# A hashed-attention and maxout kernel: softmax sums from weights added on VectorE, PSUM copies on ScalarE, and a new sharing of the PSUM banks

## The chip, the cores and the metric

The kernel runs on one core of a Trainium2 chip. The metric is device time in microseconds (us) of one execution. The profile gives the span from the first to the last instruction of one execution. The core has five engines, each with its own queue that it works through in order: TensorE (PE in the profile; PEld are its weight loads), VectorE (DVE), ScalarE (ACT), GpSimd (POOL) and SyncE (SP, which here only starts transfers). They wait for each other through semaphores. TensorE writes its products to PSUM, eight banks of 512 single-precision columns over 128 partitions; VectorE and ScalarE read them there.

## The reference

Four batches, eight heads, 768 rows, head width 64. Each row of q and k gets a bucket from the signs of six projections, and a row attends only to rows of its own bucket. A maxout layer of three products and an output product follow.

```python
q_bits = (np.einsum('bhsd,dk->bhsk', q, proj) > 0)
k_bits = (np.einsum('bhsd,dk->bhsk', k, proj) > 0)
...
mask = q_bucket[:, :, :, None] == k_bucket[:, :, None, :]
scores = np.where(mask, scale * np.matmul(q, k.transpose(0, 1, 3, 2)), -1000000000.0)
attn = np.exp(scores - np.max(scores, axis=-1, keepdims=True))
attn = attn / (np.sum(attn, axis=-1, keepdims=True) + 1e-09)
x = np.matmul(attn, v)        # to (4*768, 512)
h = np.maximum(np.maximum(x @ w1, x @ w2), x @ w3)
out = h @ w_out               # 512 -> 768 -> 512
```

## The kernel before

**The mask is in the product.** The hash bits, as plus and minus one half, stand as six or eight more rows under the 64 rows of q and k (tiles S). The score product then carries the match of the bits, and the exponential on ScalarE (L257) with a bias makes weights of unlike buckets vanish.

**Units.** The work is a loop over 192 units `u`, 48 for each batch. A unit is one head, half of the queries (384 columns) and two blocks of 128 keys: two products on TensorE (`scores`, L255) into a two-bank PSUM tile, and one exponential of 128 x 768 on ScalarE into a half-precision tile AT, of which there are 18 (`at_tiles`). Three units make the six key blocks of one head; six make a group (two heads, half of the queries).

**Order.** It is written out by hand (`manual_schedule`). In each pass of the loop stand, in this order: `scores(u + 1)`, work due at that unit (`when`), the scaling of finished groups (`steps`), one piece of the layers (`ffn.pop(0)()`), and the values and sums of finished groups (`firsts` in the first batch, `burst` every 12 units after it).

**Values and sums.** `values(g)` (L281) multiplies the weights with v, 24 products on four strips of 32 columns of the array, four at a time. `part_sums` (L337; L308 for two groups) multiplies them with ones for the row sums, again 24 products for two groups. VectorE copies the values out of PSUM (L330). `inverse` (L291 to L294, VectorE) makes reciprocals, which GpSimd spreads over partitions (L343 to L347), and L351 writes the scaled values to xT, the layers' input. A burst runs values, sums, the hash of a coming set, values, and `invert`.

**Layers.** For each half batch there are 18 first-layer groups of four products (L366), in turn for w1, w2 and w3: VectorE casts the first product to the tile ht (L370) and takes maxima with the other two (L372). Then six half groups of three products (L399) make three output blocks, which ScalarE copies out (L403); SP sends them. The pieces run one in a unit. Those of the last half batches run on after the last scores and make the tail. L385 and L387 copy the halves of the very last block.

**Inputs.** The first batch's pairs of heads come over TensorE transposes (L111, kept by VectorE at L117, placed by GpSimd at L122) and a hash (L133, L153). Later sets of four heads (`load_quad`, L170) come as four transfers, each over 32 partitions; VectorE transposes them in 32 x 32 blocks (L176, eight for a pair of sets), GpSimd narrows them to bf16 (L181), SP places them (L187), and TensorE hashes them (L197). From the third batch on GpSimd's queue issues the loads.

**PSUM.** Two score tiles of two banks (`sc_ps`), one bank for values (`av_ps`) and three banks in rotation (`ms_ps`) for all else: eight banks. Each request makes a new tile, and the framework adds the waits that its earlier use makes needful.

```python
sc_ps = ctx.enter_context(tc.tile_pool(name="sc_ps", bufs=2, space=bass.MemoryType.PSUM))
av_ps = ctx.enter_context(tc.tile_pool(name="av_ps", bufs=1, space=bass.MemoryType.PSUM))
ms_ps = ctx.enter_context(tc.tile_pool(name="ms_ps", bufs=3, space=bass.MemoryType.PSUM))
```

Of the kernel before, what the change touches and what calls it, by code (L numbers as in the profile page):

```python
# [17 lines left out]
def kernel(  # L18
# [38 lines left out]
    nat_pool = ctx.enter_context(tc.tile_pool(name="nat", bufs=6))  # L57
# [24 lines left out]
    wout_sb = konst.tile([P, NFB, DM], FP16, name="wout_sb")  # L82

# [40 lines left out]
    def pair_group(pi, side, hd):  # L124
        mp = ms_ps.tile([P, 512], FP32, tag="ms", name="mp")
        pair_keep(pi, side, hd, pair_turn(pi, side, hd, mp))

    def pair_hash(pi):
        bp = ms_ps.tile([P, 512], FP32, tag="ms", name="bp")
# [33 lines left out]
    def load_quad(side, g, xs, eng):  # L163
        if (side, g) not in nat:
            start_set((side, g), [(side, 4 * g + x) for x in range(4)])
        for x in xs:
            b, h = divmod(4 * g + x, H)
            src = (q, k)[side][b, h].rearrange("(cc t m) d -> t cc (m d)", cc=CC, t=Q)
            dst = nat[side, g][x * Q : (x + 1) * Q, :].rearrange("t (cc w) -> t cc w", cc=CC)
            eng.dma_start(dst, src)  # L170
# [7 lines left out]
    def narrow(name, u):  # L178
        if name not in t16:
            t16[name] = t16_pool.tile([P, 2, S], BF16, tag="T16", name="T16")  # L180
        nc.gpsimd.tensor_scalar(out=t16[name][:, u, :], in0=t32[name][:, u, :], scalar1=RS, scalar2=1.0,  # L181
                                op0=AluOp.mult, op1=AluOp.mult)
# [7 lines left out]
    def quad_hash(g):  # L190
        bp = ms_ps.tile([P, 512], FP32, tag="ms", name="bp")
# [8 lines left out]
        nc.vector.tensor_scalar(out=bits[:], in0=bp[:, 0:HALF], scalar1=0.0, scalar2=0.5,  # L200
                                op0=AluOp.is_gt, op1=AluOp.subtract)
# [44 lines left out]
    def scores(u):  # L246
# [5 lines left out]
        sc = sc_ps.tile([P, 2, 512], FP32, tag="sc", name="sc")  # L252
# [20 lines left out]
    def values(g):  # L273
        b, qh, jj = groups[g]
        av = av_ps.tile([P, 512], FP32, tag="av", name="av")
# [21 lines left out]
    def near(g):  # L297
        avs = []

        def part_values():  # L300
            avs.append(values(g))

        def part_sums():
            av = avs[0]
            sm = ms_ps.tile([P, 512], FP32, tag="ms", name="sm")
# [14 lines left out]
    def far(gs):  # L320
        avs, sms, sb = [], [], []

        def part_values(i):
# [4 lines left out]
            av = values(gs[i])  # L328
            avs.append(avs_pool.tile([P, HALF + 4], FP32, tag="avs", name="avs"))
            nc.vector.tensor_copy(avs[i][:, 0 : HALF + 1], av[:, 0 : HALF + 1])  # L330
            nc.gpsimd.tensor_scalar_mul(sv[:, i : i + 1], avs[i][:, HALF : HALF + 1], EPS)  # L331

        def part_sums():
            sms.append(ms_ps.tile([P, 512], FP32, tag="ms", name="sm"))
            for m in range(NM):
                for r in range(4):
                    nc.tensor.matmul(sms[0][Q * r : Q * (r + 1), 0:HALF], ones[:, :],  # L337
                                     at_of(gs[r % 2], m, r // 2)[:, 0:HALF], start=(m == 0), stop=(m == NM - 1))

        def invert():  # L340
            rb = sb[1]
# [15 lines left out]
    def ffn_groups(h):  # L357
# [3 lines left out]
        for fb in range(NFB):  # L361
            for wi in range(3):
                def go(fb=fb, wi=wi):
                    ps = ms_ps.tile([P, 512], FP32, tag="ms", name="l1")
# [3 lines left out]
                    if wi == 0:  # L368
                        hts[fb] = h_pool.tile([P, HALF], FP16, tag="ht", name="ht")
                        nc.vector.tensor_copy(hts[fb][:], ps[:, 0:HALF])  # L370
# [6 lines left out]
        def last(part, tb):  # L377
            ps = ms_ps.tile([P, 512], FP32, tag="ms", name="l2")
# [11 lines left out]
        for tb in range(MH):  # L390
            def go2(part, tb=tb):
# [3 lines left out]
                if part == 0:  # L395
                    hts["ps"] = ms_ps.tile([P, 512], FP32, tag="ms", name="l2")
# [16 lines left out]
    with tc.manual_schedule():  # L413
# [10 lines left out]
        load_quad(1, 2, range(4), nc.sync)  # L424
# [11 lines left out]
        wp = ms_ps.tile([P, 512], FP32, tag="ms", name="wp")  # L436
# [170 lines left out]
```

## Time and profile before

| | |
|---|---|
| Time, median of three runs | 284.75 us (282.47 to 287.2) |
| Span of the profiled execution | 280.6 us; its whole time is not given apart from the three above |
| TensorE busy | 270.2 us (96%), granted clock 0.998 in the mean |
| VectorE busy | 177.3 us (63%) |
| ScalarE busy | 166.2 us (59%) |
| GpSimd busy | 106.9 us (38%) |
| Read from and written to memory | 25.17 and 6.29 MB |

In the profile's groups a row gives line, engine, operation, tiles, shapes, count, then busy time and mean duration of one in ns, then the idle time ahead of these instructions and what ended most of it. Products overlap in the array: one of 384 columns is drawn 326 ns long, though the next one starts 163 ns after it, so the distance from start to start is what a product costs. In a window's row each engine has its busy us and its count of instructions; then come TensorE's granted clock, the busy share of the transfer engines, and GB/s. In a timeline row stand the start, the length, the engine, line and operation, the count of merged instructions, and in brackets the idle time before it with what released it. In the list of waits stand who waited for whom, us in total, times, and the longest.

### The profile page before, as it was taken

The page shows a single profiled execution, that of the slowest core. Times are in us where ns is not written, and L with a number is a line of the kernel's source. Part 1 is how long each engine was busy: PE and PEld are TensorE (multiplying, and loading weights), DVE is VectorE, ACT ScalarE, POOL GpSimd, SP SyncE. Part 2 cuts the span into 40 slices and gives each one's busy share as a digit, 9 for nine tenths or more (in the row PEclk, how much of TensorE's full clock was granted, in tenths as well). Part 3 has the DMA queues.
Part 4 walks back from the last instruction along what each step waited for, and adds up shares of the span by engine and source line. Part 5 has one row for each costly group of instructions (what it writes and reads, how often), then busy time and mean ns, then how long its engine had stood idle before and what let it go on. Part 6 is the DMA issues. An engine that isn't in the chain of part 4 may idle for free.

```text
span 280.6 us, 6405 instructions
## 1 busy us (share of the span) xinstructions
PE 270.2 (96%) x2482; PEld 145.9 (52%) x2482; DVE 177.3 (63%) x383; ACT 166.2 (59%) x220; POOL 106.9 (38%) x201
## 2 busy tenths in 40 slices
PE   8899989899999999999999999999999999999994
PEld 4344433454555554555555554555555555555552
DVE  3755786786536594796536594896536673568580
ACT  2686676763858484764858484864858485910102
POOL 3455958153119096543118096633021120303000
PEclk9999999999999999999999999999999999999999
DMA  7998879974117439672117349772020001200303
GB/s 231 320 183 165 127 133 230 245 101 105 42 42 200 101 50 232 180 148 70 30 70 183 85 67 225 206 122 63 1 77 37 2 1 40 75 2 0 114 0 112
DMA packets 21877, 30.99 MB, mean 110 GB/s; under 512 B 2632, under 2 KB 17368, under 8 KB 21848
## 3 DMA queue, kind: packets, MB, share of 16 engines
q0 software_dynamic: 8640, 12.59, 24.9%
q1 hardware_dynamic: 12776, 17.49, 21.7%
q10 hardware_dynamic: 432, 0.52, 0.6%
q8 instruction: 19, 0.31, 0.5%
q14 instruction: 10, 0.08, 0.1%
HBM read 25.17 MB, written 6.29 MB: 112 GB/s over the span
## 4 chain that ended last, share of the span: by engine, by line
PE 87%; DVE 6%; ACT 2%; issue 2%; DMA 1%; POOL 0%; DVEq 0%; ACTq 0%
PE l L366 31%; PE sc L255 21%; PE av L281 12%; PE l L399 10%; PE sm L337 5%; PE bp L197 3%; ACT AT L257 2%; PE mp L111 2%; PE wp L438 1%; DVE ht L372 1%; PE bp L133 1%; PE bp L153 1%; PE sm L308 1%; DMA out_dram<-osb 1%; DVE rb L294 1%
## 5 line engine op out<-in xcount | busy, mean ns | idle before, releaser
L257 ACT ACTIVATE AT<-sc 128x768 f16<-128x768 f32 x192 | 153.4, 813 | 78.2 <-PE sc L255 78.0
L366 PE MATMUL l<-xT,w_sb 128*128 128x384 f16 x576 | 113.2, 326 | 0.7 <-DVE ht L372 0.6
L255 PE MATMUL sc<-S 72*128 72x384 bf16 (+1 forms) x384 | 93.1, 326 | 3.8 <-ACT AT L257 3.0
L366 PEld LDWEIGHTS <-w_sb 128*128 128x128 f16 x576 | 55.9, 97 | 39.1 <-issue 1.2
L372 DVE TENSOR_TENSOR ht<-ht,l 128x384 f16<-128x384 f16 x96 | 52.4, 546 | 17.0 <-PE l L366 13.8
L255 PEld LDWEIGHTS <-S 72*128 72x128 bf16 (+1 forms) x384 | 35.0, 98 | 40.1 <-issue 15.6
L331 POOL TENSOR_SCALAR sv<-avs 128x1 f32<-128x1 f32 x30 | 6.4, 213 | 95.8 <-DVE avs L330 95.7
L330 DVE COPY avs<-av 128x385 f32<-128x385 f32 x30 | 16.8, 560 | 38.3 <-PE av L281 38.3
L281 PE MATMUL av<-AT,vo 128*32 128x385 f16 x768 | 37.3, 327 | 0.0
L399 PE MATMUL l<-wout_sb,ht 128*128 128x512 f16 x138 | 36.5, 379 | 0.4 <-DVE ht L372 0.4
L370 DVE CAST ht<-l 128x384 f16<-128x384 f32 x48 | 26.2, 547 | 16.0 <-PE l L366 15.2
L403 ACT COPY osb<-l 128x512 f32<-128x512 f32 x23 | 13.4, 582 | 27.2 <-PE l L399 27.2
L281 PEld LDWEIGHTS <-vo 128*32 128x32 f16 x768 | 18.6, 96 | 16.9 <-issue 8.7
L181 POOL TENSOR_SCALAR T<-T 128x768 bf16<-128x768 f32 x24 | 21.5, 894 | 13.3 <-DVE T L176 11.9
L176 DVE STREAM_TRANSPOSE T<-nat 128x384 f32<-128x384 f32 x48 | 26.2, 558 | 0.0
L399 PEld LDWEIGHTS <-ht 128*128 128x128 f16 x138 | 13.3, 97 | 13.8 <-DVE ht L372 1.8
L351 DVE SCALAR_TENSOR_TENSOR xT<-avs,sv,rb 128x384 f16<-128x384 f32 x30 | 19.7, 656 | 0.0
L337 PE MATMUL sm<-AT,ones 128*32 128x384 f16 x360 | 17.2, 326 | 0.0
L343 POOL COPY rb<-rb 128x384 f32<-128x384 f32 x15 | 7.5, 503 | 24.0 <-DVE rb L294 24.0
L122 POOL TENSOR_SCALAR S<-T 64x768 bf16<-64x768 f32 (+1 forms) x17 | 12.8, 754 | 8.0 <-DVE T L117 6.9
L347 POOL COPY rb<-rb 32x384 f32<-32x384 f32 x30 | 15.0, 500 | 1.5
L345 POOL COPY rb<-rb 32x384 f32<-32x384 f32 x30 | 15.0, 499 | 1.5
(47 smaller groups left out, 136.5 us busy)
## 6 DMA issues: line engine op xcount, KB each, us to landing
out_dram<-osb SPq DMA_DIRECT2D x23, 256.0 KB
S<-T SPq DMA_DIRECT2D x48, 96.0 KB
vo<-in_v_dram POOLq DMA_DIRECT2D x8, 384.0 KB, 6.1
nat<-in_k_dram POOLq DMA_DIRECT2D x16, 192.0 KB, 3.6
nat<-in_q_dram POOLq DMA_DIRECT2D x16, 192.0 KB, 5.8
w_sb<-in_moe_w_dram POOLq DMA_DIRECT2D x3, 768.0 KB, 9.7
nat<-in_k_dram SPq DMA_DIRECT2D x10, 192.0 KB
nat<-in_q_dram SPq DMA_DIRECT2D x8, 192.0 KB
```

The lines of the kernel that those rows point to most:

```text
L176: nc.vector.transpose(t32[name][:, u, half * HALF : (half + 1) * HALF], i_)
L181: nc.gpsimd.tensor_scalar(out=t16[name][:, u, :], in0=t32[name][:, u, :], scalar1=RS, scalar2=1.0, op0=AluOp.mult, op1=AluOp.mult)
L255: nc.tensor.matmul(sc[:, j, 0:HALF], s_of[kn][0 : D + nb, kx, m * P : (m + 1) * P], s_of[qn][0 : D + nb, qx, qh * HALF : (qh + 1) * HALF], ...
L257: nc.scalar.activation(at_tiles[u % NAT][:, :, 0:HALF], sc[:, :, 0:HALF], ActFn.Exp, bias=-SCALE * 0.25 * nb, scale=SCALE)
L281: nc.tensor.matmul(av[hd * D + w * Q : hd * D + (w + 1) * Q, 0 : HALF + 1], vt[:, x, c * D + w * Q : c * D + (w + 1) * Q], at_of(g, m, hd) ...
L330: nc.vector.tensor_copy(avs[i][:, 0 : HALF + 1], av[:, 0 : HALF + 1])
L337: nc.tensor.matmul(sms[0][Q * r : Q * (r + 1), 0:HALF], ones[:, :], at_of(gs[r % 2], m, r // 2)[:, 0:HALF], start=(m == 0), stop=(m == NM ...
L351: nc.vector.scalar_tensor_tensor(out=xt_of(gs[i]), in0=avs[i][:, 0:HALF], scalar=sv[:, i : i + 1], in1=rb[:, i, :], op0=AluOp.add, op1=Alu ...
L366: nc.tensor.matmul(ps[:, 0:HALF], w_sb[wi][:, jc, fb * P : (fb + 1) * P], xt[:, jc, :], start=(jc == 0), stop=(jc == NJC - 1))
L370: nc.vector.tensor_copy(hts[fb][:], ps[:, 0:HALF])
L372: nc.vector.tensor_tensor(out=hts[fb][:], in0=hts[fb][:], in1=ps[:, 0:HALF], op=AluOp.max)
L399: nc.tensor.matmul(ps[:, 0:DM], hts[fb][:, tb * P : (tb + 1) * P], wout_sb[:, fb, :], start=(fb == 0), stop=(fb == NFB - 1))
```

## The change

1. **Sums.** `add_weights(u)` runs on VectorE from the second batch on: the six key blocks' weights of a head are added to two blocks (two additions of 128 x 768 for each three units). The burst's sums then take 8 products instead of 24. They now stand first in the burst, followed by `invert`, the hash and the two values.
2. **ScalarE** copies the bursts' values out of PSUM (30 copies before on VectorE, of which the 24 in bursts move) and each first product (48).
3. **PSUM.** Three score tiles (`sc_banks`) up to unit 39, with `scores` two units ahead; the transposes, hashes, values and sums of that time take turns in two banks, `av_bank` and `ms_bank`. From unit 39 (`SWITCH`) two score tiles remain, one unit ahead; the third score tile's two halves and `ms_bank` form the rotation (`ring`), and `av_bank` serves the first values of each burst. `bank()` gives the next place and passes over one in `kept`, the output block under way. The tiles are made once and used all through.
4. **Sets.** `load_quad` is one transfer over 128 partitions, 24 consecutive rows of a head in each. The rows of a block therefore lie in another order, which `narrow` (GpSimd) and the hash bits' operation (VectorE) put right by strided access. There are five input buffers (`nat`) instead of six, and some units of the first batch's steps are shifted.

```diff
-    sc_ps = ctx.enter_context(tc.tile_pool(name="sc_ps", bufs=2, space=bass.MemoryType.PSUM))
-    av_ps = ctx.enter_context(tc.tile_pool(name="av_ps", bufs=1, space=bass.MemoryType.PSUM))
-    ms_ps = ctx.enter_context(tc.tile_pool(name="ms_ps", bufs=3, space=bass.MemoryType.PSUM))
+    ad_pool = ctx.enter_context(tc.tile_pool(name="adpool", bufs=6))
+    ps = ctx.enter_context(tc.tile_pool(name="ps", bufs=1, space=bass.MemoryType.PSUM))
...
+    SWITCH = 39
+    sc_banks = [ps.tile([P, 2, 512], FP32, name=f"sc{i}", tag=f"sc{i}") for i in range(3)]
+    av_bank = ps.tile([P, 512], FP32, name="av", tag="av")
+    ms_bank = ps.tile([P, 512], FP32, name="ms", tag="ms")
+    ring, kept = [av_bank, ms_bank], []
+    def bank():
+        while True:
+            ring.append(ring.pop(0))
+            if not any(ring[-1] is x for x in kept):
+                return ring[-1]
+    def switch():
+        ring[:] = [ms_bank, sc_banks[2][:, 0, :], sc_banks[2][:, 1, :]]
+    def sc_of(u):
+        return sc_banks[u % 3 if u < SWITCH else u % 2]
...
+        b, h0 = divmod(4 * g, H)
+        eng.dma_start(nat[side, g][:], (q, k)[side][b, h0 : h0 + 4].rearrange("h (t j) d -> (h t) (j d)", t=Q))
...
+    def add_weights(u):
+        g, hd, kp = unit_of(u)
+        if kp == 0:
+            return
+        t = at_tiles[u % NAT][:, :, 0:HALF]
+        if kp == 1:
+            added[g, hd] = ad_pool.tile([P, 2, HALF], FP16, tag="ad", name="ad")
+        first = added[g, hd][:] if kp > 1 else at_tiles[(u - 1) % NAT][:, :, 0:HALF]
+        nc.vector.tensor_tensor(out=added[g, hd][:], in0=first, in1=t, op=AluOp.add)
...
+            if fast:
+                nc.scalar.copy(avs[i][:, 0 : HALF + 1], av[:, 0 : HALF + 1])
...
+            n = 2 if fast else NM
+            for m in range(n):
...
-                    ps = ms_ps.tile([P, 512], FP32, tag="ms", name="l1")
+                    ps = bank()
...
-                        nc.vector.tensor_copy(hts[fb][:], ps[:, 0:HALF])
+                        nc.scalar.copy(hts[fb][:], ps[:, 0:HALF])
...
         def burst(u, gs):
-            vals, sums, invert, late = far(gs)
-            vals(0)
+            vals, sums, invert, late = far(gs, True)
             sums()
+            invert()
             hash_due(u)
+            vals(0, av_bank)
             vals(1)
-            invert()
...
-            if u + 1 < NU:
-                scores(u + 1)
+            ahead = 2 if u + 2 < SWITCH else 1
+            while told <= min(u + ahead, NU - 1):
+                scores(told)
+                told += 1
+            if u == SWITCH:
+                switch()
+            if u - 1 >= UPB:
+                add_weights(u - 1)
```

More of the change, by code (lines that the diff above doesn't have):

```diff
@@ L160, in first_bits, with load_quad @@
                                 op0=AluOp.is_gt, op1=AluOp.subtract)
[L163 to L170, printed above, removed]
+    def load_quad(side, g, eng):
+        start_set((side, g), [(side, 4 * g + x) for x in range(4)])
+        b, h0 = divmod(4 * g, H)
+        eng.dma_start(nat[side, g][:], (q, k)[side][b, h0 : h0 + 4].rearrange("h (t j) d -> (h t) (j d)", t=Q))
     def turn(name, u, half):
@@ L300, in part_values @@
         def part_values():
-            avs.append(values(g))
+            avs.append(values(g, bank()))
         def part_sums():
             av = avs[0]
-            sm = ms_ps.tile([P, 512], FP32, tag="ms", name="sm")
+            sm = bank()
             for m in range(NM):
@@ L461 @@
         first_bits(bq, 0, 0, 1)
+        scores(1)
         bps = {}
         def first_rest(side):
-            bps[side] = ms_ps.tile([P, 512], FP32, tag="ms", name="bp")
+            bps[side] = bank()
             first_hash(bps[side], side, 1)
@@ L496 @@
                 if g > 3:
-                    for x in range(4):
-                        when(need - 36 + 4 * n + x, load_quad, side, g, (x,), nc.gpsimd)
+                    when(need - 36 + 4 * n, load_quad, side, g, nc.gpsimd)
                 t0 = need - (24 if g == 2 else 21) + 4 * n
```

87 lines of the change are left out of this document (48 added, 39 removed).

## Prediction

> **What bounds the kernel now.** I read the page first, then windows, then groups by line, then the timeline of one ordinary stretch.
>
> ```profile
> span 280.6 us, 6405 instructions
> PE 270.2 (96%) x2482; PEld 145.9 (52%) x2482; DVE 177.3 (63%) x383; ACT 166.2 (59%) x220; POOL 106.9 (38%) x201
> ...
> core 0: us, PE busy (x) PEld busy (x) DVE busy (x) ACT busy (x) POOL busy (x), PEclk, DMA share, GB/s
> 8.50:52.60 44.10, 39.47 (x411) 17.92 (x410) 28.40 (x59) 30.89 (x41) 26.65 (x40) 1.00 0.96 190
> 52.60:157.00 104.40, 104.08 (x979) 57.30 (x979) 68.21 (x140) 69.20 (x91) 44.14 (x82) 1.00 0.52 118
> 157.00:245.00 88.00, 87.79 (x835) 49.14 (x828) 56.37 (x116) 58.57 (x78) 30.18 (x59) 1.00 0.31 73
> ```
>
> From 52.6 us on, TensorE (PE) is busy all but 0.5 of 192 us at granted clock 1.00: there the order of its work is the time, and each stall put into it is paid in full. Before that (the first 41 units of the loop over u) neither TensorE (39.5 of 44.1) nor ScalarE (30.9) is full. Now one ordinary unit:
>
> ```profile
> 152.15 0.82 PE L366 MATMUL l<-xT,w_sb 128*128 128x384 f16 x4
> 152.80 0.49 PE L255 MATMUL sc<-S 72*128 72x384 bf16 x2
> 153.13 0.81 PE L366 MATMUL l<-xT,w_sb 128*128 128x384 f16 x4
> ...
> 153.00 0.55 DVE L372 TENSOR_TENSOR ht<-ht,l 128x384 f16<-128x384 f16 x1 [0.43 <-PE l L366]
> ...
> 58.62 0.49 PE L255 MATMUL sc<-S 70*128 70x384 bf16 x2
> ...
> 59.20 0.81 ACT L257 ACTIVATE AT<-sc 128x768 f16<-128x768 f32 x1 [0.17 <-PE sc L255]
> ...
> 9.05 0.81 ACT L257 ACTIVATE AT<-sc 128x768 f16<-128x768 f32 x1 [1.02 <-PE sc L255]
> ...
> 9.91 0.48 PE L255 MATMUL sc<-S 70*128 70x384 bf16 x2 [0.90 <-ACT AT L257]
> ```
>
> A unit takes 0.98 us (152.15 to 153.13): 0.33 for two score products, 0.65 for a first-layer group of four. The group's last product ends at 152.97; VectorE takes it up 0.03 later and is done at 153.55. By then TensorE is 0.42 into the next group, in another bank. That overlap is what three rotating PSUM banks buy. From the last pair of rows: an ended reader releases TensorE in 0.05 us (9.86 to 9.91).
>
> **The change, part by part.**
>
> *Shorter sums: -7.8 us.*
>
> ```profile
> 155.83 1.17 PE L281 MATMUL av<-AT,vo 128*32 128x385 f16 x24
> 156.83 1.15 PE L337 MATMUL sm<-AT,ones 128*32 128x384 f16 x24
> 157.80 1.16 PE L281 MATMUL av<-AT,vo 128*32 128x385 f16 x24
> ```
>
> 24 sum products take 0.97 us (156.83 to 157.80). In the 12 bursts of the later batches 8 stay, 0.32: 12 x 0.65 = 7.8 us of TensorE saved.
>
> *Scores two ahead in the first batch: -5 us (from -13.5 to +3).*
>
> ```profile
> ACT AT L257 <- PE sc L255: 13.5, 18, 1.6
> PE sc L255 <- ACT AT L257: 3.0, 5, 0.9
> ...
> 17.76 2.92 ACT L257 ACTIVATE AT<-sc 128x768 f16<-128x768 f32 x4 [0.31 <-PE sc L255]
> ```
>
> These waits are those of the window 8.5 to 52.6. ScalarE runs dry for 13.5 us, because a values or sums block delays the next scores; back to back an exponential needs only 0.73 (four in 2.92), so 41 need 30 of the 44.1 us. A third score buffer lets it work through such a block. All 13.5 is the most. But the transposes, hashes, values and sums of this batch share two banks where they had four, and each pair's hash must still await VectorE's copies; that could cost up to the 3.0 above again. TensorE's own work here is some 33 us (41 units of scores at 0.33, ten values or sums blocks at 1.0, some 9 of transposes and hashes), so I take a good third of 13.5.
>
> *The three later banks: +36 us (17 to 40).* This is the largest term, and it comes from the built order, not from the diff's words. After unit 39 the general PSUM work turns through three places: `ms_bank` and the two halves of `sc_banks[2]`. The halves are different banks but one tile, and the framework orders accesses by the tile. I followed each product's semaphore value in the changed program to the instruction that it stands for: a product into one half waits for the VectorE or ScalarE instruction that reads the *other* half. In the old program the corresponding product waits for a reader three groups back. When two groups follow each other in the two halves, once in each turn of three, TensorE thus stands until the group just finished has been read. Scores issued behind it in its queue wait too, and the exponentials after them.
>
> ```profile
> L372 DVE TENSOR_TENSOR ht<-ht,l 128x384 f16<-128x384 f16 x96 | 52.4, 546 | 17.0 <-PE l L366 13.8
> L403 ACT COPY osb<-l 128x512 f32<-128x512 f32 x23 | 13.4, 582 | 27.2 <-PE l L399 27.2
> L385 ACT COPY osb<-l 128x256 f32<-128x256 f32 x1 | 0.4, 372 | 0.1
> 261.29 11.86 PE L366 MATMUL l<-xT,w_sb 128*128 128x384 f16 x72
> ```
>
> A wait costs: group 0.82 + 0.03 + reader 0.55 + release 0.05 = 1.45 after the group began, against 0.98 at present, so 0.47. A ScalarE copy of 384 columns I put at 0.48, between 372 ns for 256 and 582 for 512. It stands behind the unit's exponential, which starts 0.25 after the group does (59.20 against 58.95) and takes 0.81: about 0.55 lost, and 0.65 where the copy has 512 columns. In the tail no scores stand between (18 groups of four in 11.7 us, 0.65 each): 0.82 + 0.04 + 0.48 + 0.05 - 0.65 = 0.74 for a ScalarE reader, 0.8 for VectorE. Counts from the built order: 25 VectorE readers with scores between (11.8 us), 9 first copies (5.0), 6 copies of second products (3.9), 5 after values or sums (0.45 each, 2.2), 9 first copies with no scores between (6.7), 6 other such neighbours (4.8), and 9 that reach two groups back with no scores (0.15 each, 1.4). Together 36. The low end charges only what a reader's own length exceeds the scores that still fit (0.22, 0.15 and 0.25 for the first three kinds, 0.2, 0.48, 0.55 for the next): 17. The high end has VectorE busy when the product comes.
>
> *Sums behind VectorE's adds: +4 us (2 to 14).* 96 additions of 768 half-precision elements are new on VectorE; 24 value copies and 48 first-product casts leave it.
>
> ```profile
> L370 DVE CAST ht<-l 128x384 f16<-128x384 f32 x48 | 26.2, 547 | 16.0 <-PE l L366 15.2
> L330 DVE COPY avs<-av 128x385 f32<-128x385 f32 x30 | 16.8, 560 | 38.3 <-PE av L281 38.3
> L176 DVE STREAM_TRANSPOSE T<-nat 128x384 f32<-128x384 f32 x48 | 26.2, 558 | 0.0
> L351 DVE SCALAR_TENSOR_TENSOR xT<-avs,sv,rb x30: 568/611/1243, 30.7 to 258.3; 128x384 f16<-128x384 f32 x30
> L387 DVE COPY osb<-l 128x256 f32<-128x256 f32 x1 | 0.4, 424 | 3.8 <-DMA out_dram<-osb 3.8
> ```
>
> No such addition is in the trace. The rows bound it: 0.55 if two elements go at a time (as long as 384 now), 0.92 at one (547 ns plus 384 more at the 0.96 ns that lie between 256 and 384 columns). By the nearest row, L351 with two SBUF sources at one element a cycle, I take 0.92. VectorE then has 177.3 - 13.4 - 26.2 + 88 = 226 us, under the new span, so only order counts. The burst's sums now come first and need the addition of the last unit, queued on VectorE behind that unit's maximum. In six bursts that unit is a first-layer one, 0.35 each; the other six follow second-layer units, nothing. Four stretches with eight transposes (L176) in eight units lag some 0.5 each: 4.1. All 12 and the stretches in full lag give 14. The Trainium skill, "VectorE: DVE Perf Modes", section on the perf-mode tier table, gives 16-bit tensor_tensor from SBUF two elements a cycle; no row here shows it. By it the addition would be an estimated 0.56 and this term 2.
>
> ```profile
> 29.85 2.82 POOL L122 TENSOR_SCALAR S<-T 64x768 bf16<-64x768 f32 x3
> ...
> 30.74 1.24 DVE L351 SCALAR_TENSOR_TENSOR xT<-avs,sv,rb 128x384 f16<-128x384 f32 x1
> ```
>
> L351 took 1.24 rather than 0.57 while GpSimd ran L122: an addition may be held likewise, and the 14 covers it. The Trainium skill, "SBUF — State Buffer", section "Who interferes with whom", says that a VectorE instruction with two SBUF inputs contends with a GpSimd instruction that reads SBUF; the trace agrees with this 1.24.
>
> *Costed at nothing.* ScalarE gains 72 copies of 0.48 (35 us), 201 in all: below the span; in a first-layer turn it has 3 x 0.73 + 0.48 = 2.67 of 2.94 us, and without that cover each would cost its 0.48. One transfer per set over 128 partitions replaces four: 48 issues become 12 on SP's and GpSimd's queues, asked for over 30 units ahead from the third batch on; one buffer less is covered as the tile wanted was transposed a dozen units before. The strided narrowing on GpSimd may take up to double; its result is due some 13 units later. Uncovered, either costs one late set, a few us.
>
> *Sum*: 280.6 - 7.8 - 5 + 36 + 4 = 307.8 of span. The median shown, 284.75, lies 4.15 over this profile's span; with that, 312 us.
>
> **The rivals.**
> (a) *The waits across the halves are met in time*, so only the gains show: 284.75 - 7.8 - 5 + 2 = 274, faster. It decides if the reader is done before TensorE, after the group's last product and the 0.33 of scores, comes to the next group. For it: VectorE has fewer PSUM readings to do. Against it: 153.00 and 0.55 in the rows above; the reader begins when TensorE is already at 152.97. 0.07.
> (b) *VectorE becomes the second bound.* At 0.92 and held by GpSimd's reads, additions and transposes exceed the units in the four stretches (8 x 0.49 + 5.3 x 0.92 + 5.3 x 0.48 + 1.2 = 12.6 against some 9.2 us), every maximum comes late and the waits across halves grow with it: +10 beyond the term of 4, and some 8 in the waits: 330. For it: L351's 1243 ns, and the nearest row is at one element a cycle. Against it: over the whole span VectorE has 226 us of work in 308, so it catches up between stretches. 0.14. The Trainium skill's two elements a cycle (the tier table above) speak against it too; by them the stretches come to an estimated 10.7 us.
> (c) *The lookahead does all it can* (-13.5) and the waits cost the low end (17): 284.75 - 7.8 - 13.5 + 17 + 4 = 284, no change. For it: ScalarE's 13.5 us of waiting. Against: the two banks. 0.05.
>
> **How the numbers follow.** My forecast 0.74, (a) 0.07, (b) 0.14, (c) 0.05. The forecast's own range comes from the term bounds: 284.75 - 7.8 - 13.5 + 26 + 2 = 291 with the waits half way down, and 284.75 - 7.8 + 3 + 40 + 8 = 328. I give 294 to 328, which leaves (a), (c) and most of (b) out. A measurement of this kernel can tell about 2% from no change. Faster by over 2%: (a) and a bit of (c), 0.08; within 2%: the rest of (c), 0.03; slower: 0.89.
>
> **What would show each step.** In the changed profile: "PE l <- DVE ht" and "PE l <- ACT ht" among the waits with some 60 entries of 0.4 to 0.8 us, 25 to 40 us together (now 0.6); sums groups of 8 in the later bursts, 0.33 us each; first-layer work starting several us before 52.6; the additions' row at 0.55 or 0.92; ScalarE waiting less than 13.5 us in the first batch. I am wrong if TensorE's waits for readers stay under 10 us, or if first-layer work starts later than 52.6.

## The result, and the profile after

The changed kernel takes 336.06 us (median of four, 334.24 to 338.04) against 284.72 for the kernel before on the same chip: 1.1855 times as long, interval 1.1777 to 1.1934. I had said 312 us, 294 to 328. The direction was right; the loss is 51 us, where I had 27. Times and differences from here on are medians that leave out the few runs which came out longer at a lower clock.

The page after, its head, TensorE's granted clock in 40 slices, and the chain that ended last:

```profile
span 334.0 us, 6135 instructions
...
PE 279.9 (84%) x2290; PEld 144.3 (43%) x2290; DVE 202.2 (61%) x407; ACT 194.6 (58%) x292; POOL 117.2 (35%) x177
...
PEclk9769999999999979999999999979999999999999
...
PE 61%; DVE 20%; issue 8%; ACT 7%; DMA 1%; SPq 1%; DVEq 0%; ACTq 0%
```

TensorE has fewer products than before (2290 for 2482), yet it is busy for only 84% of a longer span, and VectorE now holds 20% of the chain. The waits of TensorE for readers, which were 0.6 us in the old trace, stand now in the list of waits (us in total, times, longest) and in the groups by line:

```profile
ACT AT L274 <- PE sc L272: 55.8, 92, 3.4
...
PE sc L403 <- DVE ht L409: 16.0, 24, 2.1
...
PE sc L403 <- ACT ht L407: 8.5, 18, 0.6
...
PE sc L439 <- DVE ht L409: 4.3, 4, 2.1
PE sc L439 <- ACT osb L443: 3.9, 8, 0.7
```
```profile
L403 PE MATMUL sc<-xT,w_sb 128*128 128x384 f16 x376 | 77.0, 327 | 27.2 <-DVE ht L409 16.0 <-ACT ht L407 8.5 <-ACT osb L443 1.4
...
L403 PE MATMUL ms<-xT,w_sb 128*128 128x384 f16 x200 | 41.5, 329 | 1.1 <-DVE xT L330 1.1
L197 POOL TENSOR_SCALAR T<-T 128x768 bf16<-128x768 f32 x24 | 39.2, 1634 | 28.3 <-DVE T L191 27.6
L346 DVE TENSOR_TENSOR ad<-ad,AT 128x768 f16<-128x768 f16 x48 | 34.7, 723 | 9.1 <-ACT AT L274 8.7
...
L346 DVE TENSOR_TENSOR ad<-AT,AT 128x768 f16<-128x768 f16 x48 | 28.9, 601 | 9.2 <-ACT AT L274 9.2
```

The two first-layer rows (L403) part by the tile they write: "sc", the halves of the third score tile, has 27.2 us of idle time before its products, and "ms", a bank of its own, 1.1. The line of code is the same, and so is the size of the products; what differs is the tile that they write, and so what they wait for. Two rows further down the additions (L346) come at 601 and 723 ns, and GpSimd's narrowing (L197) at 1634 ns.

Where the time went, by windows (columns as in the first window of the prediction; the first ends where the first layer starts):

```profile
8.60:56.70 48.10, 41.36 (x409) 19.42 (x410) 29.84 (x56) 30.57 (x41) 29.68 (x40) 0.89 0.78 176
56.70:161.00 104.30, 88.58 (x727) 45.70 (x726) 72.47 (x137) 65.56 (x99) 41.52 (x55) 0.98 0.40 102
161.00:300.00 139.00, 118.57 (x999) 63.76 (x997) 86.49 (x168) 89.09 (x136) 43.01 (x69) 0.99 0.21 59
```

The first layer starts at 56.7 instead of 52.6: the first batch lost 4 us, and at a granted clock of 0.89. The other 49 of the 53 us of span come later, where TensorE, full to 0.5 in 192 us before, is idle for about 15% of the time. Going from start to start of all products in the trace and taking off their streaming time, 57 us of TensorE's time after 56.6 are lost (before: about none), 52 of them ahead of products into the two halves.

One such wait, by the timeline:

```profile
65.99 0.82 PE L403 MATMUL sc<-xT,w_sb 128*128 128x384 f16 x4
...
66.64 0.49 PE L272 MATMUL sc<-S 72*128 72x384 bf16 x2
...
66.95 0.47 ACT L407 CAST ht<-sc 128x384 f16<-128x384 f32 x1
...
67.48 0.81 PE L403 MATMUL sc<-xT,w_sb 128*128 128x384 f16 x4 [0.35 <-ACT ht L407]
```

The group of 65.99 went into one half and that of 67.48 into the other. It waited for the ScalarE copy of the first half, done at 67.42, and came 1.49 us after it instead of 0.98: 0.51 lost, of which the bracket shows 0.35, because the first product after a pause also lacks the overlap with the one before it (a product is drawn 0.33 us long, and in a stream the next one starts 0.16 after it).

### The profile page after: what moved, and what is told of

Read it like the earlier page. It is cut to its first block, busy times and chain, and to the rows that moved or that the text cites. A ratio compares the mean times of both kernels' runs of the same rounds, so it can differ in the third digit from the quotient of the medians.

```text
span 334.0 us, 6135 instructions
## 1 busy us (share of the span) xinstructions
PE 279.9 (84%) x2290; PEld 144.3 (43%) x2290; DVE 202.2 (61%) x407; ACT 194.6 (58%) x292; POOL 117.2 (35%) x177
## 4 chain that ended last, share of the span: by engine, by line
PE 61%; DVE 20%; issue 8%; ACT 7%; DMA 1%; SPq 1%; DVEq 0%; ACTq 0%
PE sc L403 16%; PE sc L272 12%; DVE ht L409 9%; PE ms L403 7%; PE sc L439 5%; PE av L297 4%; PE sc L297 3%; DVE T L191 3%; ACT osb L443 3%; ACT ht L407 2%; DVE ad L346 2%; PE ms L297 2%; PE ms L439 2%; PE sc L371 1%; PE ms L213 1%
## 5 line engine op out<-in xcount | busy, mean ns | idle before, releaser
L274 ACT ACTIVATE AT<-sc 128x768 f16<-128x768 f32 x192 | 154.1, 816 | 56.4 <-PE sc L272 55.8
L403 PE MATMUL sc<-xT,w_sb 128*128 128x384 f16 x376 | 77.0, 327 | 27.2 <-DVE ht L409 16.0
L403 PEld LDWEIGHTS <-w_sb 128*128 128x128 f16 x576 | 55.9, 97 | 75.4 <-issue 41.3
L409 DVE TENSOR_TENSOR ht<-ht,sc 128x384 f16<-128x384 f16 x60 | 32.8, 547 | 43.6 <-PE sc L403 43.5
L197 POOL TENSOR_SCALAR T<-T 128x768 bf16<-128x768 f32 x24 | 39.2, 1634 | 28.3 <-DVE T L191 27.6
L403 PE MATMUL ms<-xT,w_sb 128*128 128x384 f16 x200 | 41.5, 329 | 1.1 <-DVE xT L330 1.1
L346 DVE TENSOR_TENSOR ad<-ad,AT 128x768 f16<-128x768 f16 x48 | 34.7, 723 | 9.1 <-ACT AT L274 8.7
L439 PE MATMUL sc<-wout_sb,ht 128*128 128x512 f16 x102 | 28.4, 392 | 8.5 <-DVE ht L409 4.3
L346 DVE TENSOR_TENSOR ad<-AT,AT 128x768 f16<-128x768 f16 x48 | 28.9, 601 | 9.2 <-ACT AT L274 9.2
L407 ACT CAST ht<-sc 128x384 f16<-128x384 f32 x34 | 16.3, 478 | 27.3 <-PE sc L403 27.0
L409 DVE TENSOR_TENSOR ht<-ht,ms 128x384 f16<-128x384 f16 x36 | 19.7, 547 | 20.6 <-PE ms L403 19.7
L439 PEld LDWEIGHTS <-ht 128*128 128x128 f16 x138 | 13.5, 98 | 24.8 <-issue 12.4
L297 PE MATMUL av<-AT,vo 128*32 128x385 f16 x384 | 19.0, 327 | 0.0
L141 POOL TENSOR_SCALAR S<-T 64x768 bf16<-64x768 f32 (+1 forms) x17 | 12.8, 756 | 12.7 <-DVE T L136 11.9
```

The source lines that it names most:

```text
L197: nc.gpsimd.tensor_scalar(out=t16[name][:, u, :].rearrange("p (m t cc) -> p m t cc", m=NM, cc=CC), in0=for_rows, scalar1=RS, scalar2=1.0, ...
L274: nc.scalar.activation(at_tiles[u % NAT][:, :, 0:HALF], sc[:, :, 0:HALF], ActFn.Exp, bias=-SCALE * 0.25 * nb, scale=SCALE)
L297: nc.tensor.matmul(av[hd * D + w * Q : hd * D + (w + 1) * Q, 0 : HALF + 1], vt[:, x, c * D + w * Q : c * D + (w + 1) * Q], at_of(g, m, hd) ...
L346: nc.vector.tensor_tensor(out=added[g, hd][:], in0=first, in1=t, op=AluOp.add)
L403: nc.tensor.matmul(ps[:, 0:HALF], w_sb[wi][:, jc, fb * P : (fb + 1) * P], xt[:, jc, :], start=(jc == 0), stop=(jc == NJC - 1))
L407: nc.scalar.copy(hts[fb][:], ps[:, 0:HALF])
```

## The experiments

The theory: TensorE waits because two banks are one tile, and that is most of the loss. The rivals: VectorE's additions make everything late; ScalarE's copies do; the lookahead or the sets do. All times below are medians, with ratios to the kernel before on the same chip.

### The halves, taken away and done alone

*halves_apart*: no two neighbours in the rotation are halves of one tile.

```diff
-        ring[:] = [ms_bank, sc_banks[2][:, 0, :], sc_banks[2][:, 1, :]]
+        ring[:] = [ms_bank, av_bank, sc_banks[2][:, 0, :]]
...
-            vals(0, av_bank)
+            vals(0, sc_banks[2][:, 1, :])
```

> The changed kernel with two places swapped after unit 39: the rotation takes ms_bank, av_bank and one half of the third score tile; the other half serves the first values of each burst. Only the bursts still touch both halves of one tile. Theory A (the waits across the halves, summed from the trace at some 50 us, are the loss): 282 to 292 us. Theory B (VectorE, loaded with the additions, is late and TensorE would wait anyway): over 320.

Measured: 311.91 us, 1.0972 (1.0913 to 1.1032), between the ranges of both theories. 24 us came back, so the halves are the largest single term; but 27 of the 51 us stay, and these my theory had not foreseen.

*before_shared_halves*: the old kernel, with two of its three rotating banks made as one tile.

```diff
-    ms_ps = ctx.enter_context(tc.tile_pool(name="ms_ps", bufs=3, space=bass.MemoryType.PSUM))
+    ms_ps = ctx.enter_context(tc.tile_pool(name="ms_ps", bufs=1, space=bass.MemoryType.PSUM))
+    ms_one = ms_ps.tile([P, 512], FP32, name="ms", tag="ms")
+    ms_two = ms_ps.tile([P, 2, 512], FP32, name="md", tag="md")
+    ring, kept = [ms_one, ms_two[:, 0, :], ms_two[:, 1, :]], []
```

> The kernel before, with one thing of the change: its rotation of three banks is one tile of one bank and one tile of two banks, used by halves. Theory A: 284.7 plus 30 to 50: 315 to 335, with TensorE waiting at L366 and L399 for VectorE readers of the group just before. Theory B: within 2% of 284.7.

Measured: 326.64 us (one run, so no interval) beside 283.43: some 43 us from this edit alone. Tiles made once and used all through are not the reason, for old_banks_no_additions below has them too, with separate banks, at 286.71 us. Its waits and one ordinary stretch of its timeline:

```profile
PE md L375 <- DVE ht L381: 15.7, 35, 0.7
...
PE md L375 <- DVE ht L379: 8.2, 11, 1.3
```
```profile
150.89 0.81 PE L375 MATMUL md<-xT,w_sb 128*128 128x384 f16 x4
...
151.76 0.55 DVE L381 TENSOR_TENSOR ht<-ht,md 128x384 f16<-128x384 f16 x1
...
152.36 0.81 PE L375 MATMUL md<-xT,w_sb 128*128 128x384 f16 x4 [0.33 <-DVE ht L381]
```

1.47 us from one group to the next, where 0.98 is ordinary: 0.49 lost, 0.47 predicted. The mechanism stands by itself, with no additions, no ScalarE copies and no strided access near it.

### The additions, and the old banks

*no_additions*: the changed kernel with 24 sum products from the weights themselves.

```diff
-            if u - 1 >= UPB:
-                add_weights(u - 1)
...
-            n = 2 if fast else NM
+            n = NM
```

> The changed kernel without add_weights: the bursts' sums take 24 products again. Theory A: the waits stay but are shorter, since no addition stands ahead of a reader on VectorE (0.5 instead of 0.7 us each), and the sums cost 8 more: 324 to 336. Theory B: under 300.

Measured: 326.84 us, 1.1516 (1.1435 to 1.1597): 9 us less than the changed kernel, although TensorE has 7.8 us more to do. So the additions cost some 17 us in it, not 4; a part of this is the granted clock (see the account below).

*old_banks*: the changed kernel with the PSUM plan of before.

```diff
-    sc_banks = [ps.tile([P, 2, 512], FP32, name=f"sc{i}", tag=f"sc{i}") for i in range(3)]
-    ms_bank = ps.tile([P, 512], FP32, name="ms", tag="ms")
-    ring, kept = [av_bank, ms_bank], []
+    sc_banks = [ps.tile([P, 2, 512], FP32, name=f"sc{i}", tag=f"sc{i}") for i in range(2)]
+    ms_banks = [ps.tile([P, 512], FP32, name=f"ms{i}", tag=f"ms{i}") for i in range(3)]
+    ring, kept = list(ms_banks), []
...
-        told = 2
+        told = 1
...
-            ahead = 2 if u + 2 < SWITCH else 1
+            ahead = 1
```

> The changed kernel with the PSUM of before: two score tiles, one unit ahead throughout, one bank for values, three separate banks in rotation. Additions, ScalarE copies, burst order and sets as changed. Theory A: 276 to 288 (sums 7.8 shorter, some of it lost to sums that wait for additions). Theory B: over 320. Against halves_apart it prices the lookahead of two in the first batch: if that helped, halves_apart is the faster by up to 5; if the two banks and the lower clock of that stretch cost, the slower by 4 to 8.

Measured: 302.67 us, 1.0666 (1.0584 to 1.0747), between the ranges of both theories. Without the new banks and the lookahead it is still 19 us slower than before. Two windows and one stretch of its timeline show how (these are of old_banks, as are the line numbers):

```profile
100.00:120.00 20.00, 16.02 (x133) 8.63 (x131) 16.40 (x28) 10.54 (x17) 11.96 (x16) 0.91 0.45 115
120.00:140.00 20.00, 16.66 (x122) 9.11 (x123) 17.37 (x29) 10.52 (x17) 10.01 (x10) 0.83 0.41 90
```
```profile
107.96 1.50 POOL L197 TENSOR_SCALAR T<-T 128x768 bf16<-128x768 f32 x1 [1.46 <-DVE T L191]
...
108.25 1.63 DVE L346 TENSOR_TENSOR ad<-ad,AT 128x768 f16<-128x768 f16 x1
...
110.30 0.51 DVE L409 TENSOR_TENSOR ht<-ht,ms 128x384 f16<-128x384 f16 x1
...
110.86 0.39 PE L439 MATMUL ms<-wout_sb,ht 128*128 128x512 f16 x1 [2.68 <-DVE ht L409]
...
111.37 1.74 POOL L197 TENSOR_SCALAR T<-T 128x768 bf16<-128x768 f32 x1 [1.91 <-DVE T L191]
...
111.42 0.81 PE L439 MATMUL ms<-wout_sb,ht 128*128 128x512 f16 x3
...
111.83 1.69 DVE L346 TENSOR_TENSOR ad<-ad,AT 128x768 f16<-128x768 f16 x1
...
112.16 0.10 PEld L371 LDWEIGHTS <-ones 128*32 128x32 f16 x4 [0.42 <-issue]
...
112.16 0.34 PE L371 MATMUL ms<-ad,ones 128*32 128x384 f16 x3
...
113.58 0.80 PE L371 MATMUL ms<-ad,ones 128*32 128x384 f16 x5 [1.08 <-DVE ad L346]
```

VectorE is the fuller engine in the second window (17.37 against TensorE's 16.66). An addition that starts while GpSimd narrows (L197) ends 0.4 us after the narrowing does: 107.96 + 1.50 = 109.46 and 109.88. The maximum L409 behind it is late, and TensorE, which needs that ht, stands idle for 2.7 us. Then the burst's sums, first in their burst, wait 1.08 for the next addition. The granted clock in these two windows is 0.91 and 0.83, so products also stream more slowly here.

*old_banks_no_additions*: old_banks and the edit of no_additions.

> old_banks without add_weights (sums of 24 products again); sets and ScalarE copies as changed. Theory C (an addition, with two SBUF inputs, is held on VectorE while GpSimd reads, 1.6 instead of 0.55 us, longest behind the strided narrowing): no such instruction is left but the scaling, so 282 to 290. Theory D (VectorE's sheer load): the same. Theory E (the ScalarE copies are late): still over 298.

Measured: 286.71 us, 1.0109 (1.0038 to 1.0181). What is left, the ScalarE copies and the new sets, costs 1%. So the strided sets alone are cheap; they hurt through the additions.

### Where the additions hurt: the order in the burst, and the sets

*old_banks_old_sets*: old_banks, with the sets as they were before.

```diff
-        eng.dma_start(nat[side, g][:], (q, k)[side][b, h0 : h0 + 4].rearrange("h (t j) d -> (h t) (j d)", t=Q))
+        for x in xs:
+            b, h = divmod(4 * g + x, H)
+            src = (q, k)[side][b, h].rearrange("(cc t m) d -> t cc (m d)", cc=CC, t=Q)
+            dst = nat[side, g][x * Q : (x + 1) * Q, :].rearrange("t (cc w) -> t cc w", cc=CC)
+            eng.dma_start(dst, src)
...
-        nc.gpsimd.tensor_scalar(out=t16[name][:, u, :].rearrange("p (m t cc) -> p m t cc", m=NM, cc=CC),
-                                in0=for_rows, scalar1=RS, scalar2=1.0, op0=AluOp.mult, op1=AluOp.mult)
+        nc.gpsimd.tensor_scalar(out=t16[name][:, u, :], in0=t32[name][:, u, :], scalar1=RS, scalar2=1.0,
+                                op0=AluOp.mult, op1=AluOp.mult)
```

> old_banks with the sets of before (four transfers over 32 partitions, plain narrowing at 0.9 us, plain hash bits), five buffers; the additions stay. Theory C: an addition is held at most 0.9 instead of 1.6 us, the additions' mean falls from 0.68 to about 0.6: 285 to 293. Theory D: 298 or more. Theory E: over 298.

Measured: 292.78 us, 1.0306 (1.0219 to 1.0393): the strided sets cost 9.9 us where the additions are. The edit puts back transfers, narrowing and hash bits together; that it is the narrowing is read from the later additions of each head (ad<-ad,AT), which fall from 758 ns in the mean to 621.

*old_banks_old_sets_values_first* moves the first values ahead of the sums and `invert` behind the second values; *copies_only* is the same with 24 sum products and no additions, so that of the whole change only ScalarE's copies stay. In both, second values of a burst can be written to the bank of its sums before `inverse` reads it, so some reciprocals are made from other numbers; the prices below rest on the two kernels after them.

```diff
-            sums()
-            invert()
-            hash_due(u)
-            vals(0, av_bank)
+            vals(0, av_bank)
+            sums()
+            hash_due(u)
             vals(1)
+            invert()
```

> old_banks_old_sets with the burst order of before (values, sums, hash, values, inverse), so that 1 us of values covers the last addition. If the sums wait for additions at each burst: 3 to 8 us under old_banks_old_sets, 278 to 288, at best under the kernel before by most of the 7.8 us of sums. If not: the same as old_banks_old_sets within 2.

> old banks, old sets, no additions, old burst order: what is left of the change are the ScalarE copies, five input buffers and a few shifted units in the first batch. Theories C and D: 281 to 287, as before. Theory E: 290 or more.

Measured: 285.06 us, 1.0056 (1.0021 to 1.0091), and 285.89, 1.0085 (1.0041 to 1.0129). In *values_before_sums* and *copies_only_in_order*, the same two otherwise, `invert` stands right behind the sums:

```diff
-            sums()
-            invert()
-            hash_due(u)
-            vals(0, av_bank)
+            vals(0, av_bank)
+            sums()
+            invert()
+            hash_due(u)
             vals(1)
```

> old_banks_old_sets with the burst in the order values, sums, inverse, hash, values: 1 us of values stands between the last unit and the sums that need its addition. If bursts wait for the last addition: 284 to 288 against 292.8. If the rest of the loss of old_banks_old_sets is readers late on VectorE in the transposing stretches: within 3 of 292.8.

> As values_before_sums, without additions (sums of 24 products): of the change only the ScalarE copies, five input buffers and some shifted units are left. 283 to 287 if the copies are free on ScalarE; 290 or more if exponentials come late behind them.

Measured: *values_before_sums* 283.12 us, 0.9979 (0.9948 to 1.001); *copies_only_in_order* 284.19, 1.0069 (1.0032 to 1.0106). From old_banks_old_sets to values_before_sums 9.7 us are gained by putting one block of 24 products, 1 us, ahead of the sums. A wait in the list of old_banks_old_sets, which that of values_before_sums no longer has:

```profile
PE ms L373 <- DVE ad L348: 3.8, 6, 0.9
```

The groups by line of values_before_sums:

```profile
L348 DVE TENSOR_TENSOR ad<-ad,AT 128x768 f16<-128x768 f16 x48 | 28.8, 600 | 3.5 <-ACT AT L276 3.2
...
L200 POOL TENSOR_SCALAR T<-T 128x768 bf16<-128x768 f32 x24 | 21.3, 887 | 21.9 <-DVE T L195 20.9
```

The narrowing is back at 887 ns and the held additions at 600 instead of 758 in old_banks. But of the 7.8 us that shorter sums save, 1.1 reach the end.

### The lookahead without the halves

*lookahead_apart*: the new banks with the rotation of halves_apart, old sets, no additions, the burst in the order of values_before_sums. Against copies_only_in_order it has the new banks and the lookahead alone. The lines of the rotation and of the burst, against the changed kernel:

```diff
-        ring[:] = [ms_bank, sc_banks[2][:, 0, :], sc_banks[2][:, 1, :]]
+        ring[:] = [ms_bank, av_bank, sc_banks[2][:, 0, :]]
...
-            sums()
-            invert()
-            hash_due(u)
-            vals(0, av_bank)
+            vals(0, sc_banks[2][:, 1, :])
+            sums()
+            invert()
+            hash_due(u)
             vals(1)
```

> copies_only_in_order with the score tiles of the change: three tiles and two units ahead up to unit 39 with two banks for all else, later two score tiles and a rotation of ms_bank, av_bank and one half of the third tile, the other half for the bursts' first values. It prices the first batch alone. If the lookahead gains: 277 to 283. If two banks and the lower clock eat it up, as the first-layer start at 56.7 in the changed profile says: 288 to 294.

Measured: 293.0 us, 1.0331 (1.0277 to 1.0386), 8.8 us over copies_only_in_order. Its first batch, by window:

```profile
8.60:56.40 47.80, 40.29 (x409) 19.01 (x410) 28.25 (x57) 30.59 (x41) 26.60 (x40) 0.93 0.86 175
```

The first layer starts at 56.4 against 54.2 in copies_only_in_order: the lookahead with two general banks loses here too. The rest comes later: 5.3 us of lost product time against 0.5, by the same sum from start to start. Nearly all of these 5 us stand ahead of the burst's sums and first values: one half of the third score tile is still in the rotation while the other takes burst values.

### Does it help anywhere, and a last test of the sets

*additions_where_free*: values_before_sums, with no additions (and 24 sum products) in the four bursts whose stretches hold the transposes of coming sets.

```diff
+    LATE = (6, 7, 10, 11)
...
-        if kp == 0:
+        if kp == 0 or g // 2 in LATE:
             return
...
-            n = 2 if fast else NM
+            short = fast and gs[0] // 2 not in LATE
+            n = 2 if short else NM
...
```

> values_before_sums with additions for 8 of the 12 bursts alone; the four bursts after units with eight VectorE transposes sum 24 products as before. 8 x 0.65 = 5.2 us of TensorE saved with little wait: 278 to 283, faster than before and than the change. If additions are held by GpSimd's reads wherever they stand: 284 or more.

Measured: 279.43 us, 0.988 (0.985 to 0.991): 1.2% faster than the kernel before, clear of its interval, but under the 2% that I had set for calling a kernel faster. By line and by window:

```profile
L349 DVE TENSOR_TENSOR ad<-ad,AT 128x768 f16<-128x768 f16 x32 | 17.8, 555 | 1.4 <-ACT AT L276 1.3
```
```profile
52.00:157.00 105.00, 102.86 (x934) 56.35 (x930) 68.61 (x145) 80.08 (x123) 46.69 (x82) 1.00 0.52 119
157.00:245.00 88.00, 87.08 (x788) 48.39 (x777) 56.17 (x119) 69.75 (x109) 32.74 (x59) 1.00 0.30 73
```

An addition that nothing holds takes 0.55 us, and TensorE is nearly full again (idle 3.1 of 193 us). Eight short bursts should save 5.2 us; 3.6 are there against the kernel before, 4.8 against copies_only_in_order. The four bursts left out have both the eight transposes on VectorE and GpSimd's narrowing beside them; this run doesn't part the two.

Two more kernels put the shifted units of the first batch back, in additions_where_free and in copies_only_in_order:

```diff
...
-        far_at((0, 1), (10, 13))
-        far_at((2, 3), (22, 25))
-        near_at(4, 31)
-        near_at(5, 37)
+        far_at((0, 1), (10, 12))
+        far_at((2, 3), (22, 24))
+        near_at(4, 30)
+        near_at(5, 36)
...
```

> additions_where_free with the first batch's steps at the units of before. First-layer work started at 54 us with the shifted units and at 52.6 before, with one stretch at half clock about 12 us. If the shifted units are the cause: 277 to 278.5. If not: 279.4 as before the edit.

> copies_only_in_order with the first batch's steps at the units of before; what is left of the change are the ScalarE copies and five input buffers. If the shifted units are what it loses: 282.5 to 283.3, as before. If the ScalarE copies cost the 1: 284.3.

Measured: 280.85 us, 0.9899 (0.986 to 0.9937), and 285.83, 1.0065 (1.0032 to 1.0098). The shifted units are not the 0.7% that copies_only_in_order loses.

*changed_old_sets*: the changed kernel with the old sets only.

> The changed kernel with the sets of before (four transfers, plain narrowing and hash bits), five buffers. If holding the additions lengthens the readers across the halves: 322 to 328, the waits at L403 on VectorE nearer 0.5 than 0.7 us each. If the strided sets only cost where banks are apart: 334 or more.

Measured: 327.98 us, 1.1534 (1.1468 to 1.1599): 8 us less than the changed kernel. The strided sets are paid in the full change, too, but hardly at the place that I expected: the waits at L403 on VectorE fall from 0.67 only to 0.63 us each.

## Why the prediction was right and wrong

One chain of kernels, each a step from the last, gives a price for each part. The prices are not independent: what one wait hides, the next step shows.

| step | us | my term |
|---|---|---|
| ScalarE's copies (copies_only_in_order, 284.19 against 283.02) | +1 | 0 |
| additions and short sums, values first, plain sets (283.12) | -1 | part of -7.8 + 4 |
| sums first in the burst (292.78) | +10 | part of -7.8 + 4 |
| strided sets (302.67) | +10 | 0 |
| two general banks, lookahead, halves not neighbours (311.91) | +9 | -5 |
| neighbouring halves (336.06) | +24 | +36 |

The kernels ran on several chips; the kernel before took 283.0 to 283.4 us beside those of the table and 284.7 beside the changed kernel.

A part of these prices is the granted clock, which my prediction left at 1.00. In the 69 executions of the kernel before that ran beside the experiments, the time follows it: 283.0 us in the mean at a clock of 1.00, 284.9 at 0.994, 287.7 at 0.988. A kernel's time, times what its mean clock lacks to 1, is an estimate of this part, and a high one, since TensorE also waits while its clock is low: 2.0 us in values_before_sums, 3.1 in old_banks_old_sets, 10.7 in old_banks (clock 0.965), 11.9 in halves_apart, 8.9 in the changed kernel (0.974), 4.0 in changed_old_sets, 3.4 in no_additions. By this estimate some 8 of the strided sets' 10 us in the table are a lower clock and not the waiting itself, and so are 5 of the 8 us that changed_old_sets gains and 5 of the 9 that no_additions gains.

**Right in place and kind, too small in size: the halves.** The place, the reader and the size of a wait were as worked out: 0.49 and 0.51 lost in the two ordinary cases, for 0.47 and 0.55. The list of waits has the entries that I named as the sign, 54 with 33 us together in the four rows shown above, for "some 60" and "25 to 40". The term of 36 lies between what the halves cost alone (43, with the first batch in it) and what their parting gives back in the full change (24, since late readers then stall products in the other banks). But in the changed trace 52 us are lost ahead of the halves, more than my high end of 40: the 41 groups that follow scores lose 0.69 each, for the 0.49 I had in the mean (19.0 for 39); the 26 with no scores between lose 12.2 together, for 12.9 in my list. A few very long waits, up to 2.1 us for VectorE's maxima, make the first number: the high end, "VectorE busy when the product comes", which I had as an edge of the range.

**Right: the sums' own saving, and the ScalarE copies.** The short sums:

```profile
87.67 0.51 PE L371 MATMUL ms<-ad,ones 128*32 128x384 f16 x8
88.00 1.16 PE L297 MATMUL av<-AT,vo 128*32 128x385 f16 x24
```

They take 0.33 us, as predicted. The 72 copies hide behind other work but for 1 to 2 us (copies_only_in_order and copies_only_old_units).

**Wrong: "The strided narrowing may take up to double ... costed at nothing".** It took 1.83 times as long (1634 for 894 ns), within the doubling I allowed, and its own result was in time. I looked only at who waits for the narrowing, not at who is held while it reads. In the same list I had a VectorE instruction at 1.24 us instead of 0.57 beside a GpSimd operation, put this into the additions' range and into rival (b), and never connected it with the doubled narrowing. The strided sets cost 8 to 10 us, the lower clock included. In the changed trace itself:

```profile
198.94 1.74 POOL L197 TENSOR_SCALAR T<-T 128x768 bf16<-128x768 f32 x1 [1.91 <-DVE T L191]
...
199.40 1.69 DVE L346 TENSOR_TENSOR ad<-ad,AT 128x768 f16<-128x768 f16 x1
```

The Trainium skill, "SBUF — State Buffer", section "Who interferes with whom", tells that a VectorE instruction with two SBUF inputs contends with one of GpSimd's that reads SBUF; this 1.69 for an addition of 0.55 agrees.

**Wrong: "Sums behind VectorE's adds: +4 us (2 to 14)".** Net of the 7.8 saved, additions and order came to about +8.5 with plain sets, so the term was some 16, over my high end. I had the wait of the sums at 0.35 in six bursts and nothing in the other six, from the additions' place in the queue on an idle VectorE. The 9.7 us for the order alone are 0.8 for each of the 12 bursts in the mean. By the sum from start to start, eight of the 12 bursts of old_banks_old_sets lose 0.4 to 1.4 us ahead of their sums, some 7.6 together (0.9 in values_before_sums), and the output products behind late maxima some 2 more than there. That the addition takes 0.55 and not the 0.92 I chose (nearest row L351, one element a cycle) would have made the term smaller; the Trainium skill's two elements a cycle ("VectorE: DVE Perf Modes", the perf-mode tier table) agree with the 555 ns of the undisturbed additions. So rival (b) is what came nearest, 330 us: not through the length of an addition but through additions held by GpSimd, and the waits across halves did grow with it, as (b) says (at L403 16.0 us on VectorE's maxima, against 9.8 in no_additions).

**Wrong: "Scores two ahead in the first batch: -5 us".** The first layer started 4.1 us later, not earlier, which I had named as a sign of being wrong, and ScalarE's waits in that window rose from 13.5 to 18.5 us:

```profile
ACT AT L274 <- PE sc L272: 18.5, 20, 3.3
...
PE ms L213 <- DVE xT L330: 2.4, 1, 2.4
```
```profile
15.58 0.90 PE L130 MATMUL av<-iden,nat 128*128 128x128 f32 x3 [1.23 <-DVE S L177]
```
```profile
12.00:22.00 10.00, 8.77 (x36) 4.11 (x34) 4.45 (x8) 4.36 (x6) 3.41 (x6) 0.50 0.81 193
```

The rows of L213 and of 15.58 are the cost that I had named and sized at up to 3.0: a hash and a transpose wait for one of the two banks, still to be read by VectorE. The wait of the hash for xT, 1.7 to 2.4 us, is in all five kernels with the new banks and in none with the old ones. The window from 12 to 22 us I had not thought of: the granted clock is 0.50 for 10.2 us from 11.8 on, where the old trace has 1.00. The other profiles part the two, as far as they go. With the banks of before and the shifted units, the first layer starts 0.2 and 0.7 us late where 3.4 us ahead of it run at half clock (additions_where_free, old_banks_no_additions), and 1.6 late where 6.8 us do (copies_only_in_order, values_before_sums). With the new banks it starts 2.4 late at 3.4 us of half clock (no_additions), 3.8 at 6.8 (lookahead_apart), 4.1 and 4.4 at 10.2 (changed kernel, halves_apart) and 8.5 at 17.0 (changed_old_sets). So at the same clock the two banks with the lookahead cost some 2 us, where I had a gain of 5, about the length of the hash's wait, and the lower clock makes the rest. This is from one profile of each kernel, and those with no half clock there scatter by 2 us (old_banks 0.5 early, old_banks_old_sets 0.8 and additions_where_free_old_units 1.7 late). What brings the clock down in this part was not tried.

**The sum.** My four terms gave +27. With +8.5 for sums and additions in place of -3.8, +10 for the sets, +9 for banks and lookahead in place of -5, the halves that remain (+24) and 1 for the copies, it is 52 or 53 over the 283 to 284 of before.

## What to carry to other kernels

Two banks that are read by different instructions should be two tiles: made as halves of one, each group waits for the reader of its neighbour, and a reader that is late for any reason is then paid at once. When work is moved to VectorE next to a full TensorE, count not its length but what is queued behind it, and what GpSimd reads at that time; the additions gained, 1.0 and 1.2%, only in the two kernels in which no GpSimd narrowing ran beside them and the sums did not come first. An operation "costed at nothing" because its own result is early still needs the question which other engine it holds up. And a difference of two times holds the granted clock too, so compare the clocks of both kernels before a price is put down to a wait.

## What the runs showed of the hardware

- The granted clock fell to 0.50 in steps of 3.4 us in the middle of a busy kernel (changed kernel at 121.0 and 220.0, each for 3.4 us, after TensorE had stood idle for 2.1 us; old_banks at 112.8 and 184.5, after idle times of 2.7 us). One idle time of 2.4 us, at 48.7 in the changed kernel, was not followed by such a stretch. The Trainium skill, "TensorE: Matmul & The Clock Gate", section "A second HAM failure mode: psum-queue depth-cycling", tells of a kernel in which frequent short idle times between groups of products make the clock swing between half and full; the trace agrees in that idle times of 2 to 3 us go ahead of the swing, but they are single ones here. A stall can thus cost more than its length: by estimate up to 1.7 us more for each such stretch, half of its 3.4.
- GpSimd's narrowing of 128 x 768 elements with strided access took 1634 ns instead of 894, and the hash bits of 384 columns, read and written with a stride, on VectorE 1017 instead of 557. Without any additions (old_banks_no_additions) the narrowing takes 1602, so the length is its own:

```profile
L216 DVE TENSOR_SCALAR bits<-ms 128x384 bf16<-128x384 f32 x3 | 3.0, 1017 | 0.6 <-PE ms L213 0.6
```
